# Two pairs of batch 1 prepared during batch 0's attention, and element-wise work moved from GpSimd to VectorE

## The chip, the core and the metric

The kernel runs on one core of one Trainium2 chip. The metric is the device time of one execution in microseconds (us). A core has TensorE (PE in the profile; its weight loads are PEld), VectorE (DVE), ScalarE (ACT), GpSimd (POOL) and SyncE (SP), which here issues most of the DMAs. Each engine works through its own instructions in order; semaphores make one engine wait for another.

## The reference, cut to what matters

Three layers run one after the other on 2 batches of 768 tokens. The first is a linear attention with a decaying state (8 heads of 48), the second adds the real part of a two-dimensional Fourier transform and a normalised two-layer network, the third is a gated network with a mixing over tokens.

```
for t in range(S):                                   # attention, per batch and head
    cur = np.einsum('bhd,bhe->bhde', u[None] * kt, vt)
    y[:, :, t] = np.einsum('bhd,bhde->bhe', rt, state + cur)
    state = wt[:, :, :, None] * state + np.einsum('bhd,bhe->bhde', kt, vt)
...
X = np.fft.fft(np.fft.fft(x, axis=1), axis=2)        # first network
u = x + np.real(X)
un = (u - mean(u)) / np.sqrt(var(u) + 1e-06)
x = u + np.maximum(un @ w_ch1, 0.0) @ w_ch2
...
h = gelu(x @ w_in); u, v = halves(h)                 # second network
v_n = (v - mean(v)) / np.sqrt(var(v) + 1e-06) * g_ln
out = x + (u * (w_sg @ v_n + b_sg)) @ w_out
```

## The kernel before, in words

**Pairs.** Attention is done for a pair of heads at a time: n = 0 to 3 are the pairs of batch 0, n = 4 to 7 those of batch 1. A pair's 768 tokens are cut in 6 chunks of 128. `prep` loads a pair (decays into `P`, receptance and key into `rk`, values into `v`) and makes the scaled operands: the running product of the decays is a scan on VectorE (L232), its reciprocal comes from a logarithm and an exponential on ScalarE (L238, L239), then follow four products over 112x768: receptance (L245), key (L247), a check sum (L249) and a correction of the key (L250). The rooms of odd pairs are called `prk`, `XE` and `XO`, those of even pairs `P` and `rk`.

**Own term.** Each token's own contribution `dv` is values times a number per head, `dg`. For batch 0 `dg` is a matmul into PSUM (`dg_ps`) of the product made in L243, copied by ScalarE (L274). For batch 1 it is two products of 128x576 (L264, L266) and a reduction on VectorE (L267). L279 multiplies the values by it.

**Chain of a pair.** TensorE makes scores (`sc_ps`) and transposes the keys (`kn_ps`). ScalarE copies both; GpSimd masks the scores (L294, 128x384). The keys' copy `kn` goes into products with the values (`kv_ps`), ScalarE copies these (L316), a scan on VectorE turns them into chunk states (L319) with the decays that ScalarE spread out into `dec` (L317), ScalarE writes the states `U` (L321), TensorE makes `y_ps`. L344 adds `dv`. `butterfly` (L349, L350) adds and subtracts the halves of the sequence and splits the result in a high part on ScalarE (L351) and a low part (L352). The keys' copy, the chunk states and the butterfly share one buffer, `kn`.

**Weights.** They come as 64-bit numbers. `convert` makes 32-bit ones on VectorE (L170 to L172), `divide` rounds to a high part on ScalarE (L176) and subtracts for a low part `w` (L177). Matmuls run three passes over high and low parts.

**Stages.** Batch 0's attention comes first, then its Fourier transform. Then `merge` weaves batch 1's attention and transform with the first network on batch 0 (`z_ps`, `ch`; L531 makes the low part `z_lo`). From then on the first network on batch 1 and the second network follow. A scheduler orders each engine's instructions; `first_through` is the last VectorE instruction of batch 0's transform, and batch 1's scans, its first own products and the later weights' conversions are held behind it. `NP` is 4. In `attention` the line that calls `prep` ahead is L374 to L376: two pairs ahead, but only within the same batch. `KV` and `PV` name the pairs whose key product and own product are on VectorE rather than GpSimd; `TM` are the pairs whose own term is made of products.

## Time and profile before

| | before |
|---|---|
| median of 3 runs | 485.19 us (483.95 to 487.18) |
| the profiled execution: its time | 485.52 us |
| the profiled execution: its span | 483.7 us |
| mean granted TensorE clock | 0.947 |
| PE / PEld busy | 433.6 us (90%) / 408.3 us (84%) |
| DVE busy | 274.0 us (57%), 453 instructions |
| ACT busy | 172.7 us (36%) |
| POOL busy | 182.1 us (38%), 182 instructions |

The span is what the trace covers; 1.8 us of the execution lie around it. Busy shares are means over stages that differ: between 14.5 and 76.5 us is batch 0's attention, to 104.1 us its transform, to 216 us batch 1's attention woven with the first network, and from there TensorE is busy almost without a break.

### The profile page before, as it was taken

The page shows a single profiled execution, that of the slowest core. Times are in us where ns is not written, and L with a number is a line of the kernel's source. Part 1 is how long each engine was busy: PE and PEld are TensorE (multiplying, and loading weights), DVE is VectorE, ACT ScalarE, POOL GpSimd, SP SyncE. Part 2 cuts the span into 40 slices and gives each one's busy share as a digit, 9 for nine tenths or more (in the row PEclk, how much of TensorE's full clock was granted, in tenths as well). Part 3 has the DMA queues.
Part 4 walks back from the last instruction along what each step waited for, and adds up shares of the span by engine and source line. Part 5 has one row for each costly group of instructions (what it writes and reads, how often), then busy time and mean ns, then how long its engine had stood idle before and what let it go on. Part 6 is the DMA issues. An engine that isn't in the chain of part 4 may idle for free.

```text
span 483.7 us, 6884 instructions
## 1 busy us (share of the span) xinstructions
PE 433.6 (90%) x2662; PEld 408.3 (84%) x2662; DVE 274.0 (57%) x453; ACT 172.7 (36%) x369; POOL 182.1 (38%) x182
## 2 busy tenths in 40 slices
PE   8778788876789688999999799999998999999994
PEld 8667787765678678899999699999987998999994
DVE  4857387389986978634044963541158734711332
ACT  2435355452344236444322532431355413311110
POOL 2857553154786967320000341200446524200330
PEclk9659899897979989999999899999999999999998
DMA  8948534036035223013000041000243100110002
GB/s 213 251 146 265 166 119 130 0 101 242 0 119 176 91 67 110 1 40 91 1 0 2 1 131 33 1 0 1 66 114 88 61 1 1 43 56 1 0 20 87
DMA packets 14074, 36.75 MB, mean 76 GB/s; under 512 B 1808, under 2 KB 5680, under 8 KB 13648
## 3 DMA queue, kind: packets, MB, share of 16 engines
q1 hardware_dynamic: 13456, 32.54, 22.5%
q0 software_dynamic: 576, 3.68, 2.2%
q8 instruction: 23, 0.38, 0.3%
q14 instruction: 19, 0.16, 0.1%
HBM read 33.86 MB, written 2.36 MB: 75 GB/s over the span
## 4 chain that ended last, share of the span: by engine, by line
PE 55%; DVE 15%; issue 10%; POOL 6%; DMA 5%; ACT 4%; SPq 1%; POOLq 0%; ACTq 0%; DVEq 0%
PE s_ps L107 10%; PE ch L107 8%; PE z_ps L107 8%; PE o_ps L107 5%; PE u_ps L107 4%; PE d_ps L107 3%; PE x_ps L107 3%; PE v_ps L107 3%; PE t_ps L426 2%; PE y_ps L342 2%; DMA raw<-in_wsg 2%; DVE st L171 2%; DVE st L170 2%; DVE st L172 1%; DMA w_raw<-in_w 1%
## 5 line engine op out<-in xcount | busy, mean ns | idle before, releaser
L107 PE MATMUL ch<-z_hi,w 128*128 128x384 f32 x288 | 84.5, 355 | 3.9 <-DVE uT L541 2.3
L107 PE MATMUL z_ps<-us_hi,w 128*128 128x384 f32 x288 | 82.5, 348 | 0.8 <-ACT us_hi L506 0.5
L107 PEld LDWEIGHTS ch<-z_hi,w 128*128 128x128 f32 x288 | 55.4, 199 | 6.0 <-ACT z_hi L530 2.7
L107 PE MATMUL ch<-z_lo,w 128*128 128x384 f32 x144 | 51.3, 356 | 10.2 <-DVE z_lo L531 10.2
L531 DVE SCALAR_TENSOR_TENSOR z_lo<-z_ps,z_hi 128x384 fp32r<-128x384 f32 x48 | 26.4, 552 | 55.7 <-ACT z_hi L530 55.7
L107 PEld LDWEIGHTS z_ps<-us_hi,w 128*128 128x128 f32 x288 | 54.1, 193 | 2.2 <-ACT us_hi L506 0.8
L107 PE MATMUL z_ps<-us_lo,w 128*128 128x384 f32 x144 | 49.4, 343 | 0.0
L530 ACT ACTIVATE z_hi<-z_ps 128x384 fp32r<-128x384 f32 x48 | 23.4, 490 | 57.0 <-PE z_ps L107 43.8
L107 PEld LDWEIGHTS ch<-z_lo,w 128*128 128x128 f32 x144 | 28.5, 198 | 12.4 <-DVE z_lo L531 12.1
L623 POOL TENSOR_TENSOR vn_lo<-t_g,vn_hi 128x384 fp32r<-128x384 f32 x16 | 16.1, 1014 | 57.1 <-ACT vn_hi L622 57.1
L619 DVE SCALAR_TENSOR_TENSOR t_g<-s_ps,g,bsg 128x384 f32<-128x384 f32 x16 | 9.5, 615 | 43.6 <-PE s_ps L107 43.6
L294 POOL TENSOR_SCALAR_AFFINE_SELECT sc<-sc 128x384 f32<-128x384 f32 x32 | 29.5, 939 | 12.0 <-ACT sc L293 12.0
L342 PE MATMUL y_ps<-v,sc 128*128 128x120 f32 (+1 forms) x192 | 34.0, 301 | 0.0
L177 POOL TENSOR_TENSOR w<-st,w 128x384 fp32r<-128x384 f32 (+1 forms) x18 | 24.4, 1363 | 24.0 <-ACT w L176 23.9
L107 PE MATMUL s_ps<-wsg_hi,vn_lo 128*128 128x384 f32 x96 | 32.3, 336 | 0.0
L107 PE MATMUL s_ps<-wsg_hi,vn_hi 128*128 128x384 f32 x96 | 32.3, 336 | 0.0
L107 PE MATMUL s_ps<-wsg_lo,vn_hi 128*128 128x384 f32 x96 | 32.3, 336 | 0.0
L483 POOL TENSOR_TENSOR z_lo<-uc,z_hi 128x384 fp32r<-128x384 f32 x7 | 7.8, 1120 | 60.0 <-ACT z_hi L482 59.9
L342 PEld LDWEIGHTS y_ps<-v,sc 128*128 128x128 f32 x192 | 28.6, 209 | 1.2 <-issue 0.8
L107 PEld LDWEIGHTS z_ps<-us_lo,w 128*128 128x128 f32 x144 | 27.9, 194 | 0.0
L177 POOL TENSOR_TENSOR wsg_lo<-raw,wsg_hi 128x384 fp32r<-128x384 f32 x12 | 12.4, 1038 | 33.2 <-ACT wsg_hi L176 33.2
L622 ACT CAST vn_hi<-t_g 128x384 fp32r<-128x384 f32 x16 | 8.0, 513 | 38.9 <-DVE t_g L620 28.0
(261 smaller groups left out, 1060.0 us busy)
## 6 DMA issues: line engine op xcount, KB each, us to landing
raw<-in_w SPq DMA_DIRECT2D x12, 384.0 KB, 3.4
w_raw<-in_w SPq DMA_DIRECT2D x12, 384.0 KB, 4.5
raw<-in_win SPq DMA_DIRECT2D x8, 384.0 KB, 3.8
prod<-in_ruk SPq DMA_DIRECT2D x4, 624.0 KB, 4.6
tdft<-in_tdft POOLq DMA_DIRECT2D x2, 1158.0 KB, 6.8
v<-in_v SPq DMA_DIRECT2D x8, 288.0 KB, 5.7
raw<-in_wsg SPq DMA_DIRECT2D x12, 192.0 KB, 2.4
out<-o SPq DMA_DIRECT2D x12, 192.0 KB, 1.9
```

The costliest lines, as they stand in the source:

```text
L107: nc.tensor.matmul(o, lhsT=x, rhs=y, start=start and i == 0, stop=stop and i == len(ps) - 1, **kw)
L170: behind(nc.vector.tensor_scalar(out=st, in0=top, scalar1=3, scalar2=0x3FFFFFF8, op0=ALU.logical_shift_left, op1=ALU.bitwise_and), first_t ...
L171: nc.vector.scalar_tensor_tensor(out=st, in0=top, scalar=0xC0000000, in1=st, op0=ALU.bitwise_and, op1=ALU.bitwise_or)
L177: nc.gpsimd.tensor_tensor(out=w.lo[to], in0=x, in1=w.hi[to].bitcast(F32), op=ALU.subtract)
L294: nc.gpsimd.affine_select(out=sc, in_=sc, pattern=[[0, 3], [1, C]], compare_op=ALU.is_gt, fill=0.0, base=0, channel_multiplier=-1)
L342: nc.tensor.matmul(y3[:, i, to], lhsT=sc[h][:, i, :], rhs=vf[:, of], start=c == 0, stop=True, skip_group_check=c > 0)
L426: nc.tensor.matmul(o, lhsT=l, rhs=r, start=i == 0, stop=i == len(parts) - 1)
L530: nc.scalar.activation(out=z.hi, in_=z_ps, func=AF.Relu)
L531: nc.vector.scalar_tensor_tensor(out=z.lo, in0=z_ps, scalar=0.0, in1=z.hi.bitcast(F32), op0=ALU.max, op1=ALU.subtract)
L619: nc.vector.scalar_tensor_tensor(out=t, in0=s_ps[h], scalar=g[:, f:f + 1], in1=bsg[:, hs], op0=ALU.mult, op1=ALU.add)
L622: nc.scalar.copy(vn.hi[:, f, 3 * h:3 * h + 3], th)
L623: nc.gpsimd.tensor_tensor(out=vn.lo[:, f, 3 * h:3 * h + 3], in0=th, in1=vn.hi[:, f, 3 * h:3 * h + 3].bitcast(F32), op=ALU.subtract)
```

## The change

It does six things.

1. The first two pairs of batch 1, n = 4 and 5, are prepared during batch 0's attention: `prep` may now run past the batch's end (the loop's last bound is `len(pairs)`, and n = 2 and 3 look three pairs ahead), and only scans from n = 6 on (`NP + AP`), and own products from n = 5 on, stand behind `first_through`. That needs a fourth `ends` buffer.
2. All key products (L247 before) are on VectorE; before, those of n = 2 to 7 were on GpSimd.
3. Batch 1's own products (L264, L266 before) are on VectorE, and so is the product with the values (L279) of all pairs. For batch 0 it reads `dg_ps` in PSUM directly; the copy by ScalarE is gone.
4. The low parts of all weights (L177 before) are on VectorE.
5. `dec` has no buffer of its own any more: it lies beside the chunk states in the `kn` buffer and is written 112x288 wide, so it can be written only after the `kv_ps` matmuls have read `kn`.
6. GpSimd keeps the masks, batch 0's products of pairs 1 to 3 in L243, the butterflies' low parts and small work of the networks.

```diff
-KV = range(2)
+KV = range(8)
+AP = 2
-PV = range(1)
+PV = (0, *range(4, 8))
...
     def divide(w, to, x):
         nc.scalar.copy(w.hi[to], x)
-        nc.gpsimd.tensor_tensor(out=w.lo[to], in0=x, in1=w.hi[to].bitcast(F32), op=ALU.subtract)
+        nc.vector.tensor_tensor(out=w.lo[to], in0=x, in1=w.hi[to].bitcast(F32), op=ALU.subtract)
...
-            if b:
+            if n >= NP + AP:
                 behind(scan, first_through)
...
-        ends = all_ends[n % 3]
+        ends = all_ends[n % 4]
...
             own = (nc.vector if n in PV else nc.gpsimd).tensor_tensor(out=r, in0=r, in1=k, op=ALU.mult)
-            behind(own, first_through, mybir.DependencyClass.Sync)
-            nc.gpsimd.tensor_tensor(out=r, in0=r, in1=u.to_broadcast([C, NC_, 2 * D]), op=ALU.mult)
+            if n >= NP + AP - 1:
+                behind(own, first_through)
+            nc.vector.tensor_tensor(out=r, in0=r, in1=u.to_broadcast([C, NC_, 2 * D]), op=ALU.mult)
...
-        nc.scalar.copy(dg[:, :, :, 0], dg_ps[:, :2 * NC_].rearrange("p (c h) -> p c h", h=2))
-        times_v(dv, dg, v)
+        times_v(dv, dg_ps[:, :2 * NC_].rearrange("p (c h o) -> p c h o", h=2, o=1), v)
...
     def times_v(dv, dg, v):
-        nc.gpsimd.tensor_tensor(out=dv.rearrange("p c (h e) -> p (c h) e", h=2), in0=v.rearrange("p c (h e) -> p (c h) e", h=2),
+        nc.vector.tensor_tensor(out=dv.rearrange("p c (h e) -> p (c h) e", h=2), in0=v.rearrange("p c (h e) -> p (c h) e", h=2),
...
-        us = ap([PR, D, NC_], "kn")
+        both = ap([PR, 2, D, NC_], "kn")
+        us, dec = both[:, 0], both[:, 1]
+        nc.scalar.copy(dec, ends[:, None, :].to_broadcast([PR, D, NC_]))
         nc.scalar.copy(us, kv_ps[:, :NC_ * D].rearrange("p (c e) -> p e c", c=NC_))
-        nc.scalar.copy(dec[:, :, 0:NC_ - 1], ends[:, None, 0:NC_ - 1].to_broadcast([PR, D, NC_ - 1]))
...
-            for m in range(len(ready) + n, min(n + (3 if n == 0 else 2), (b + 1) * NP)):
+            for m in range(len(ready) + n, min(n + (3 if n in (0, NP - 2, NP - 1) else 2), len(pairs))):
```

The scheduler makes new orders of this. Line numbers after the change are 2 or 3 higher than before. On VectorE in the middle of batch 0's attention the order before was this, from pair 3's scan (`XO`) on; `kn` are chunk states and butterflies of the pairs before it:

```order
L232 SCALAR_TENSOR_TENSOR XO<-XO,d_91 112x774
L319 SCALAR_TENSOR_TENSOR kn<-kn,dec 112x288
L344 TENSOR_TENSOR dv<-y_ps,dv 128x288
L245 SCALAR_TENSOR_TENSOR XO<-XO 112x768
L349 TENSOR_TENSOR kn<-dv 128x288
L350 TENSOR_TENSOR kn<-dv 128x288
L344 TENSOR_TENSOR dv<-y_ps,dv 128x288
L249 SCALAR_TENSOR_TENSOR y_379,unit<-XO,y_379 112x768
L250 SCALAR_TENSOR_TENSOR XO<-y_379,XO 112x768
L319 SCALAR_TENSOR_TENSOR kn<-kn,dec 112x288
L344 TENSOR_TENSOR dv<-y_ps,dv 128x288
```

After the change pair 4 (`P`, `rk`) and its own products (`prod`) stand there, ahead of and around the next chunk states:

```order
L252 SCALAR_TENSOR_TENSOR XO<-y_377,XO 112x768
L234 SCALAR_TENSOR_TENSOR P<-P,d_91 112x774
L347 TENSOR_TENSOR dv<-y_ps,dv 128x288
L247 SCALAR_TENSOR_TENSOR rk<-rk,P 112x768
L249 TENSOR_TENSOR rk<-rk,y_396 112x768
L251 SCALAR_TENSOR_TENSOR y_396,unit<-P,y_396 112x768
L266 TENSOR_TENSOR prod<-prod 128x576
L322 SCALAR_TENSOR_TENSOR kn<-kn 112x288
L252 SCALAR_TENSOR_TENSOR rk<-y_396,rk 112x768
L269 TENSOR_TENSOR prod<-prod 128x576
```

So pair 3's next chunk states no longer follow its keys directly: pair 4's scan and products come in between.

The second place is VectorE at the start of the woven stage, right after batch 0's last transform rows (`uT`). Before, it was pair 4 that was prepared there:

```order
L232 SCALAR_TENSOR_TENSOR P<-P,d_91 112x774
L671 TENSOR_TENSOR unit<-unit 112x1
L496 TENSOR_TENSOR uc<-uT_84 128x384
L531 SCALAR_TENSOR_TENSOR z_lo<-z_ps,z_hi 128x384
L245 SCALAR_TENSOR_TENSOR rk<-rk,P 112x768
L531 SCALAR_TENSOR_TENSOR z_lo<-z_ps,z_hi 128x384
L497 TENSOR_TENSOR uc<-uc,uT_84 128x384
L267 TENSOR_REDUCE dg<-prod 128x12
L170 TENSOR_SCALAR st<-w_raw 128x768
```

After, the scan there is pair 6's, the two products `prod` are pair 5's own term, and the low part of a weight (L179) follows its conversion at once:

```order
L234 SCALAR_TENSOR_TENSOR P<-P,d_91 112x774
L266 TENSOR_TENSOR prod<-prod 128x576
L674 TENSOR_TENSOR unit<-unit 112x1
L499 TENSOR_TENSOR uc<-uT_84 128x384
L269 TENSOR_TENSOR prod<-prod 128x576
L500 TENSOR_TENSOR uc<-uc,uT_84 128x384
L534 SCALAR_TENSOR_TENSOR z_lo<-z_ps,z_hi 128x384 x2
L270 TENSOR_REDUCE dg<-prod 128x12
L172 TENSOR_SCALAR st<-w_raw 128x768
L281 TENSOR_TENSOR dv<-v,dg 128x576
L173 SCALAR_TENSOR_TENSOR st<-w_raw,st 128x768
L174 SCALAR_TENSOR_TENSOR st<-w_raw,st 128x768
```

The first `z_lo` now has two products more ahead of it, and pair 4's products are gone from this place.

## Rows read from the trace of the kernel before

**Rows 1.** Windows: us; busy (xcount) PE, PEld, DVE, ACT, POOL; PEclk; DMA share, GB/s
```profile
14.50:76.50 62.00, 50.35 (x383) 44.23 (x383) 43.26 (x53) 27.00 (x59) 39.77 (x36) 0.81 0.63 187
...
104.10:193.70 89.60, 68.61 (x432) 60.25 (x432) 77.92 (x89) 35.92 (x74) 63.87 (x42) 0.90 0.37 122
193.70:216.00 22.30, 21.12 (x166) 19.73 (x165) 11.62 (x27) 9.60 (x21) 6.36 (x8) 1.00 0.02 2
```

**Rows 2.** Waits of PE, 104.1 to 193.7 us: total us, times, longest us
```profile
PE ch L107 <- DVE z_lo L531: 9.7, 5, 3.0
PE sc_ps L290 <- DVE rk L250: 4.7, 1, 4.7
```

**Rows 3.** Waits of DVE in the same stretch
```profile
DVE st L170 <- POOL w L177: 5.1, 4, 2.8
```

**Rows 4.** Timeline of DVE: start us, us, then the instruction
```profile
105.97 1.29 DVE L671 TENSOR_TENSOR unit<-unit 112x1 f32<-112x1 f32 x1
...
116.66 0.94 DVE L250 SCALAR_TENSOR_TENSOR rk<-y,rk 112x768 f32<-112x768 f32 x1
...
168.32 2.92 DVE L250 SCALAR_TENSOR_TENSOR rk<-y,rk 112x768 f32<-112x768 f32 x1
```

**Rows 5.** Timeline of POOL
```profile
104.44 2.80 POOL L264 TENSOR_TENSOR prod<-prod 128x576 f32<-128x576 f32 x1 [0.83 <-DVE uT L459]
...
208.67 0.99 POOL L294 TENSOR_SCALAR_AFFINE_SELECT sc<-sc 128x384 f32<-128x384 f32 x2 [1.50 <-ACT sc L293]
```

**Rows 6.** Groups of DVE, 104.1 to 193.7 us: form, xcount | busy us, mean ns | idle before
```profile
L171 DVE SCALAR_TENSOR_TENSOR st<-w_raw,st 128x768 uint32<-128x768 uint32 x6 | 8.4, 1406 | 0.1
...
L531 DVE SCALAR_TENSOR_TENSOR z_lo<-z_ps,z_hi 128x384 fp32r<-128x384 f32 x12 | 6.6, 546 | 1.4 <-ACT z_hi L530 1.4
L170 DVE TENSOR_SCALAR st<-w_raw 128x768 uint32<-128x768 uint32 x6 | 6.5, 1078 | 2.3 <-POOL w L177 2.3
...
L232 DVE TENSOR_TENSOR_SCAN prk<-prk,d 112x774 f32<-112x774 f32 x2 | 3.5, 1758 | 0.0
```

**Rows 7.** Groups of POOL in the same stretch that stay on POOL
```profile
L294 POOL TENSOR_SCALAR_AFFINE_SELECT sc<-sc 128x384 f32<-128x384 f32 x12 | 12.4, 1050 | 2.5 <-ACT sc L293 2.5
...
L352 POOL TENSOR_TENSOR AL<-kn,AH 128x576 fp32r<-128x576 f32 x2 | 3.5, 1772 | 3.3 <-ACT AH L351 3.3
L483 POOL TENSOR_TENSOR z_lo<-uc,z_hi 128x384 fp32r<-128x384 f32 x2 | 2.1, 1072 | 2.4 <-ACT z_hi L482 2.4
```

**Rows 8.** Groups of ACT, 104.4 to 205 us
```profile
L176 ACT CAST w<-st 128x768 fp32r<-128x768 f32 x6 | 5.0, 832 | 17.2 <-DVE st L172 17.2
...
L317 ACT COPY dec<-ends 112x240 f32<-112x240 f32 x4 | 1.5, 383 | 0.0
```

**Rows 9.** Waits of DVE, 14.5 to 76.5 us
```profile
DVE dv L344 <- PE y_ps L342: 9.7, 3, 5.3
DVE kn L319 <- ACT kn L316: 3.7, 1, 3.7
```

**Rows 10.** Groups of DVE, 14.5 to 76.5 us
```profile
L232 DVE TENSOR_TENSOR_SCAN prk<-prk,d 112x774 f32<-112x774 f32 x1 | 4.5, 4483 | 0.0
...
L247 DVE TENSOR_TENSOR prk<-prk,AL 112x768 f32<-112x768 f32 x1 | 2.5, 2500 | 0.9 <-ACT AL L239 0.9
...
L352 DVE TENSOR_TENSOR AL<-kn,AH 128x576 fp32r<-128x576 f32 x1 | 0.8, 757 | 0.5 <-ACT AH L351 0.5
```

**Rows 11.** Groups of POOL, 14.5 to 76.5 us, that leave POOL
```profile
L279 POOL TENSOR_TENSOR dv<-v,dg 128x576 f32<-128x576 f32 x4 | 5.3, 1328 | 1.8 <-DVE kn L350 1.8
L177 POOL TENSOR_TENSOR w<-st,w 128x384 fp32r<-128x384 f32 x4 | 4.5, 1135 | 4.3 <-ACT w L176 4.3
...
L247 POOL TENSOR_TENSOR XO<-XO,y 112x768 f32<-112x768 f32 x1 | 1.5, 1540 | 0.0
```

**Rows 12.** Windows of two later stretches, columns as in rows 1
```profile
260.00:279.00 19.00, 15.75 (x81) 14.37 (x81) 17.93 (x38) 8.94 (x21) 5.60 (x5) 0.91 0.01 1
360.00:380.00 20.00, 18.20 (x100) 17.10 (x99) 17.93 (x34) 11.45 (x24) 11.94 (x17) 1.00 0.36 99
```

More of the change, by code (lines that the diff above doesn't have):

```diff
@@ L850, in fused @@
         states = [sh.tile([PR, NC_ - 1, 2 * D], F32, name=f"U{i}") for i in range(2)]
-        all_ends = [sh.tile([PR, NC_], F32, name=f"ends{i}") for i in range(3)]
-        dec = sh.tile([PR, D, NC_], F32, name="dec")
-        for t in (*states, *all_ends, dec):
+        all_ends = [sh.tile([PR, NC_], F32, name=f"ends{i}") for i in range(4)]
+        for t in (*states, *all_ends):
             nc.gpsimd.memset(t, 0.0)
```

## The prediction

> **What bounds the kernel now.** The page's slices come first: TensorE is busy nearly everywhere after 216 us, so a change to other engines can only pay ahead of that. The windows view then cuts the front into stages [rows 1]. From 104.1 to 193.7 us, where batch 1's four pairs are prepared beside the first network, VectorE is busy 77.9 of 89.6 us and TensorE 68.6, at a mean granted clock of 0.90: VectorE is the fuller one. The waits view shows which way it goes: TensorE stands 9.7 us for `z_lo`, which VectorE makes late, and 4.7 us for pair 4's keys [rows 2]. VectorE itself stands 5.1 us for GpSimd's low parts, which must be read before the conversion buffer can be written again [rows 3]. From 193.7 to 216 us TensorE is busy 21.1 of 22.3 us. In batch 0's attention, 14.5 to 76.5 us, VectorE is busy 43.3 of 62 us, and its long waits are for `y_ps` (9.7 us) and for the copy of `kv_ps` (3.7 us) [rows 1, 9]: there it is a link in the pairs' chain, not full.
>
> The second thing to see is that VectorE's busy time is not all work. The same product takes 0.94 us at 116.66 and 2.92 us at 168.32 [rows 4]. L671, one number per partition, takes 1.29 us, and it ends just when GpSimd's L264 (104.44 to 107.24) does [rows 4, 5]. So the two engines hold each other up. I set each VectorE group of the stretch against its shortest instance (0.94 for 768 wide, 1.75 for a scan). L171 has 6 instances at 1.41, which gives 2.7 us too much (shortest 0.95), L170 6 at 1.08 against its shortest, 0.53, gives 3.3 [rows 6]. Over the 16 groups that show it that makes 23.5 us of the 77.9. The same working gives 13.0 us of 43.3 in batch 0's attention, of which pair 1's scan (4.48 against 1.75) and key product (2.50 against 0.94) are 4.3 [rows 10].
>
> **The change part by part.**
>
> *The woven stage, 104.1 to 193.7.* Undisturbed, VectorE's work there is 77.9 - 23.5 = 54.4 us. By the two orders it loses two preparations (2 scans of 1.75, 6 products of 0.94), one reduction, one `z_lo` and one half conversion: 3.5 + 5.7 + 0.75 + 0.55 + 0.55, about 11.1. It gains 6 low parts 768 wide and 2 of 384, 2 key products, 6 own products and 3 products with the values. These VectorE has not done before in these forms, so their price goes by width: 0.94 for 768 [rows 4], 0.55 for 384 [rows 6], and 0.76 for 576, the time of the one butterfly low part that VectorE makes [rows 10]. That makes 5.6 + 1.1 + 1.9 + 4.6 + 2.3, about 15.3. Net +4.2, so 58.6 us. What GpSimd still costs: before, 63.9 us of its busy time went with 23.5 us of excess, 0.37 us per us. Of its groups masks, low parts of butterflies and column sums stay, 12.4 + 3.5 + 2.1 = 18.0 us [rows 7], so 18.0 x 0.37 = 6.6 us. VectorE would be busy 65.2 us.
>
> Its idle time was 89.6 - 77.9 = 11.7 us. The 5.1 us of waits for GpSimd go. New ones come: at two places a low part follows its conversion at once, so VectorE, in order, stands for ScalarE's cast of 0.83 us [rows 8], and everything behind it, `z_lo` among it, stands too: +1.7. Idle 8.3, the stretch 73.5 us, a gain of 16.1. This is above the 68.6 us that TensorE was busy there, so TensorE does not bind yet; the floor of this term is a gain of 89.6 - 68.6 = 21. What is late next is `z_lo` again, at the start, with two own products ahead of it.
>
> *Batch 0's attention.* VectorE undisturbed has 43.3 - 13.0 = 30.3 us. Added are pair 4 and 5's preparations (2 scans, 6 products: 9.1), 4 key products (3.8; two of them pair 4's and 5's), 3 instructions of pair 4's own term (2.3), 4 products with the values (3.0), and 4 low parts of 384 whose casts fall ahead of the end (2.2): 20.4, so 50.7. GpSimd loses 5.3 + 4.5 + twice 1.5 [rows 11] and keeps 27 of its 39.8 us; at 13.0 / 39.8 = 0.33 us per us that is 8.8 of excess. VectorE would be busy 59.5 of the old 62 us. Before, 18.7 us were idle. The waits of 9.7 and 3.7 us [rows 9] are the cover under which pairs 4 and 5 hide; they are real time in the chain of the pairs, so part of them remains. `dec` now waits for `kv_ps` and stands on the chain, about 0.4 us for each of 4 pairs [rows 8]. With 6 us left idle the stretch is 65.5, with 10 it is 69.5. I take 7.5: 67, or +5. Bounds: nothing added if the chain is shortened by the GpSimd work that leaves it; +16 if the old idle time all stays.
>
> *DMAs.* Pair 4's and 5's loads are issued in this stage either way (the order of SP has the same loads, one 338 KB load of `P` earlier); nothing is priced.
>
> *The transform, 76.5 to 104.1, and 193.7 to 216.* TensorE leads there and the added low parts (4 and 2 of 0.55) fall where VectorE waits: zero, with 1 us as the bound.
>
> *From 216 on.* 18 to 22 low parts of 384 move to VectorE. It has room except in two stretches where it is busy 17.9 of 19 us and 17.9 of 20 us, and TensorE stands beside it (15.8 and 18.2 busy) [rows 12]. In the first 4 low parts (2.2 us) come in front of the sums that free `ch`, while some GpSimd interference leaves. In the second 6 low parts (3.3 us) and a conversion that stood later come ahead of the last `vn_lo`, with 2.1 us idle to take them. I take +2; bounds -1 and +5.
>
> Sum against the profiled execution's own 485.5: +5 - 16 + 2 = -9, so **476.5 us**. The median of the runs shown is 0.3 lower than that execution, which is within what they scatter.
>
> A rule weighed: GpSimd's remaining masks run against a VectorE that now has far more two-input instructions. The rows give 0.37 us of hold-up per us of GpSimd [rows 1, 7]. The Trainium skill, "SBUF — State Buffer", section "Who interferes with whom", says that a VectorE instruction with two SBUF inputs and a GpSimd instruction that reads SBUF share a port under an exclusive lock, held for the whole instruction, and that the loser blocks fully. By that rule the remaining 18 and 27 us could cost VectorE up to 1 us each instead of 0.37 and 0.33, and the sum would be about 506. The rows agree in kind (L671 above), but not with a collision every time.
>
> **The rivals.** *Most of it comes back in batch 0 (same).* VectorE stands in order for each `y_ps` and copy as before, so 14 us stay idle there instead of 7.5: 73.5 us, +11.5, and 485.5 + 11.5 - 16 + 2 = 483. For it: those waits come from the pairs' chain, not from GpSimd. Against it: before, pair 2's products stood behind the longest one, 5.3 us [rows 9], and by the new order its key product and correction come earlier.
>
> *The masks hold up a full VectorE (slower).* One mechanism, both stages: as VectorE rests less, each us of GpSimd costs it r instead of 0.35. The time is 476.5 + 45 (r - 0.35), with 45 = 18 + 27 us left on GpSimd. It equals the old time at r = 0.55 and is 1% slower from r = 0.66, so 491 or more. For it: the rule above, and pair 1's scan, stretched from 1.75 to 4.48 under continuous GpSimd work [rows 10]. Against it: a mask undisturbed is 0.5 us [rows 5], half its busy mean, so the measured 18 us are already stretched.
>
> *More than that (faster).* VectorE's idle time falls to 4 in the woven stage and TensorE sets the pace: -20.5; batch 0 +2.5; later 0: 467.5.
>
> That the change does not do what it says can be left out: the orders show pairs 4 and 5 in batch 0's attention and no low part of a weight on GpSimd.
>
> **How the numbers follow.** Forecast (470 to 480.3) 0.55, more than that 0.07, most comes back 0.25, slower 0.13. About 1% is what a measurement of this kernel can tell from no change: faster is 0.55 + 0.07 = 0.62, within 1% is 0.25, slower 0.13. The range runs from the better rival, 467, into the case of "same", 488; above it lies most of the slower rival, below it little.
>
> **What would show it.** Right: GpSimd busy near 90 us (half), VectorE's L250 near 0.94 in the woven stage, pair 4's scores before the first `ch`, the stretch from batch 0's last transform row to pair 7's keys near 74 us, batch 0's attention ending 3 to 8 us later. Wrong: that stretch above 82 us with VectorE busy above 75 (the masks), or above 82 with VectorE idle 12 or more (the chain); batch 0's attention 12 us later; a new wait of TensorE in the last 270 us beyond 5 us.

## The result and the profile after

The changed kernel takes **469.51 us** (median; 467.92 to 474.93) against 485.05 for the kernel before: a ratio of 0.9694, with an interval of 0.961 to 0.978. Measured once more beside other kernels it took 470.67 us, ratio 0.970 (0.964 to 0.976). The forecast was 476.5 us with a range of 467 to 488: the direction was right, the time lies in the range, and the gain of 15.5 us is larger than the 9 that were summed.

| | before | after |
|---|---|---|
| profiled execution: time / span | 485.52 / 483.7 us | 468.76 / 466.8 us |
| mean granted TensorE clock | 0.947 | 0.958 |
| TensorE busy / idle in the span | 433.6 / 50.1 us | 427.9 / 38.9 us |
| VectorE busy | 274.0 us | 284.0 us |
| GpSimd busy | 182.1 us | 93.7 us |

GpSimd lost 88 us of busy time, and VectorE, which took that work, got only 10 more. The windows view of the changed kernel (us; busy (xcount) of PE, PEld, DVE, ACT, POOL; granted clock; DMA share, GB/s) has batch 0's attention, the woven stretch up to pair 7's keys, and what follows up to batch 1's first transform row; the first two answer to [rows 1]:

```profile
15.40:78.60 63.20, 49.10 (x382) 43.26 (x382) 57.16 (x81) 30.87 (x64) 26.51 (x25) 0.87 0.65 195
106.82:174.58 67.76, 58.75 (x407) 52.16 (x405) 62.39 (x96) 30.07 (x60) 13.55 (x15) 0.95 0.44 147
174.58:225.20 50.62, 50.45 (x330) 48.99 (x330) 20.30 (x45) 21.36 (x51) 8.29 (x9) 0.93 0.11 32
```

The woven stretch fell from 89.4 to 67.8 us, and GpSimd is busy 13.6 us in it instead of 63.9. Its waits (total us, times, longest), first of TensorE, then of VectorE, answering to [rows 2, 3]:

```profile
PE ch L109 <- DVE z_lo L534: 5.5, 4, 3.2
```

```profile
DVE w L179 <- ACT w L178: 2.5, 2, 1.6
DVE rk L247 <- DMA rk<-in_rk: 1.2, 1, 1.2
DVE prk L234 <- DMA prk<-in_wx: 0.7, 1, 0.7
DVE prod L266 <- DMA prod<-in_ruk: 0.4, 1, 0.4
```

TensorE's wait for pair 4's keys is gone, that for `z_lo` fell from 9.7 to 5.5. VectorE's wait for GpSimd's low parts is gone too; in its place it stands 2.5 us for ScalarE's casts and 2.3 us for loads. VectorE's timeline shows the two key corrections of the stretch (0.94 and 2.92 before, [rows 4]) and the product of one number per partition that took 1.29 us before:

```profile
109.14 0.15 DVE L674 TENSOR_TENSOR unit<-unit 112x1 f32<-112x1 f32 x1
...
147.96 0.94 DVE L252 SCALAR_TENSOR_TENSOR rk<-y,rk 112x768 f32<-112x768 f32 x1
...
173.64 0.94 DVE L252 SCALAR_TENSOR_TENSOR prk<-y,prk 112x768 f32<-112x768 f32 x1
```

All kernels below are cut at the same four events on VectorE: the low part of batch 0's last butterfly (end of **S1**), batch 0's last transform row (**S2**), pair 7's corrected keys (**S3**, the woven stretch), and the end (**S4**). "Hold-up" is one measure for all: each VectorE instruction's time less that of the shortest instance of its line and shape in any run, summed over S1 (from 15 us) and S3. The names are those of the experiments. The medians are of all executions; the ratios leave out, as slow, executions over 1.5% above the fastest of their kernel: one of one_early (678.6 us at a mean clock of 0.556), one of late_low_back_same, three of the kernel before beside the first four experiments, and the one of low_back_same that its stages are read from.

| kernel | median us | ratio (95%) | S1 | S2 | S3 | S4 | hold-up S1, S3 | GpSimd busy S1, S3 |
|---|---|---|---|---|---|---|---|---|
| before | 485.05 | 1 | 76.4 | 27.9 | 89.4 | 290.0 | 11.2, 25.0 | 39, 64 |
| after | 469.51 | 0.969 (0.961 to 0.978) | 78.6 | 28.2 | 67.8 | 292.2 | 8.6, 6.8 | 27, 14 |
| after_again | 470.67 | 0.970 (0.964 to 0.976) | 81.7 | 28.1 | 68.2 | 293.4 | 8.3, 6.5 | 30, 14 |
| early_only | 486.64 | 1.0055 (1.002 to 1.009) | 90.3 | 28.0 | 74.5 | 293.0 | 18.7, 18.1 | 49, 50 |
| no_early | 475.10 | 0.977 (0.969 to 0.985) | 72.4 | 27.8 | 86.7 | 288.6 | 7.0, 5.9 | 25, 17 |
| low_back_same | 475.50 | 0.976 (0.966 to 0.985) | 82.9 | 28.2 | 70.1 | 294.4 | 8.1, 10.3 | 32, 28 |
| products_back_same | 480.76 | 0.990 (0.982 to 0.998) | 86.0 | 28.9 | 70.4 | 293.5 | 16.6, 15.6 | 47, 35 |
| late_low_back_same | 470.49 | 0.966 (0.958 to 0.975) | 80.0 | 28.2 | 68.4 | 292.8 | 8.9, 6.6 | 30, 15 |
| extra_two | 478.96 | 0.988 (0.982 to 0.994) | 86.5 | 27.8 | 70.0 | 293.1 | 14.4, 10.2 | 47, 33 |
| extra_one | 474.60 | 0.980 (0.974 to 0.986) | 81.3 | 28.3 | 69.1 | 293.9 | 9.9, 7.8 | 46, 30 |
| one_early | 472.47 | 0.976 (0.969 to 0.983) | 72.5 | 28.0 | 75.4 | 290.4 | 7.0, 4.4 | 26, 16 |
| pairs_off | 463.72 | 0.956 (0.949 to 0.962) | 76.2 | 28.3 | 65.5 | 292.3 | 2.7, 4.1 | 18, 12 |
| masks_left | 459.27 | 0.950 (0.942 to 0.958) | 74.2 | 28.5 | 65.0 | 291.1 | 2.8, 2.9 | 18, 8 |
| masks_no_early | 470.34 | 0.970 (0.965 to 0.975) | 70.6 | 28.0 | 82.4 | 289.7 | 2.5, 3.4 | 12, 12 |

The stages come from one execution each (and GpSimd's times in S1 from 15 us on), and S1 must be read with care. after_again is the changed kernel once more:

> The changed kernel once more, beside the runs it is compared with. Both theories: 468 to 472, batch 0's attention 78 to 80 us, the woven stretch 67 to 69.

Here is the whole of S1 in the two executions, first after, then after_again:

```profile
0.00:78.60 78.60, 60.15 (x465) 53.75 (x465) 66.61 (x96) 35.55 (x73) 31.01 (x43) 0.89 0.69 201
```

```profile
0.00:81.70 81.70, 65.72 (x465) 59.31 (x465) 66.71 (x96) 35.70 (x73) 33.74 (x43) 0.81 0.65 193
```

The same 465 matmuls take 60.2 us at a granted clock of 0.89 and 65.7 at 0.81, and S1 is 3.1 us longer, above the 78 to 80 that were expected. S3 repeats within half a microsecond.

### The profile page after: what moved, and what is told of

Read it like the earlier page. It is cut to its first block, busy times and chain, and to the rows that moved or that the text cites. A ratio compares the mean times of both kernels' runs of the same rounds, so it can differ in the third digit from the quotient of the medians.

```text
span 466.8 us, 6863 instructions
## 1 busy us (share of the span) xinstructions
PE 427.9 (92%) x2662; PEld 405.1 (87%) x2662; DVE 284.0 (61%) x517; ACT 173.0 (37%) x365; POOL 93.7 (20%) x118
## 5 line engine op out<-in xcount | busy, mean ns | idle before, releaser
L109 PE MATMUL ch<-z_hi,w 128*128 128x384 f32 x288 | 82.8, 348 | 5.3 <-ACT z_hi L533 2.8
L109 PE MATMUL z_ps<-us_hi,w 128*128 128x384 f32 x288 | 81.5, 344 | 0.0
L296 POOL TENSOR_SCALAR_AFFINE_SELECT sc<-sc 128x384 f32<-128x384 f32 x32 | 25.4, 812 | 66.4 <-ACT sc L295 66.3
L109 PEld LDWEIGHTS ch<-z_lo,w 128*128 128x128 f32 x144 | 28.3, 196 | 8.7 <-DVE z_lo L534 8.7
L345 PE MATMUL y_ps<-v,sc 128*128 128x120 f32 (+1 forms) x192 | 32.4, 296 | 0.0
L345 PEld LDWEIGHTS y_ps<-v,sc 128*128 128x128 f32 x192 | 27.6, 205 | 0.9 <-issue 0.7
L109 PE MATMUL x_ps<-tdft,AH 128*128 128x386 f32 (+1 forms) x72 | 19.3, 350 | 6.0 <-ACT AH L354 6.0
L109 PEld LDWEIGHTS x_ps<-tdft,AH 128*128 128x128 f32 x72 | 13.0, 192 | 6.5 <-ACT AH L354 6.5
```

Of the source, the lines that this page charges most:

```text
L109: nc.tensor.matmul(o, lhsT=x, rhs=y, start=start and i == 0, stop=stop and i == len(ps) - 1, **kw)
L296: nc.gpsimd.affine_select(out=sc, in_=sc, pattern=[[0, 3], [1, C]], compare_op=ALU.is_gt, fill=0.0, base=0, channel_multiplier=-1)
L345: nc.tensor.matmul(y3[:, i, to], lhsT=sc[h][:, i, :], rhs=vf[:, of], start=c == 0, stop=True, skip_group_check=c > 0)
```

## The experiments

### Which part of the change pays

Two theories stood against each other. *Relief*: VectorE is the bound of the woven stretch; GpSimd's work stretches its instructions, so taking that work off and taking two preparations out each help there, and what the second costs in batch 0's attention depends on GpSimd. *Early preparation is the whole gain* was the main rival.

**early_only**: the early preparation alone (`AP` is 2), every operation on its old engine.

```diff
-            if b:
+            if n >= NP + AP:
                 behind(scan, first_through)
...
-            behind(own, first_through, mybir.DependencyClass.Sync)
+            behind(own, first_through if n >= NP + AP - 1 else None, mybir.DependencyClass.Sync)
...
-            for m in range(len(ready) + n, min(n + (3 if n == 0 else 2), (b + 1) * NP)):
+            for m in range(len(ready) + n, min(n + (3 if n in (0, NP - 2, NP - 1) else 2), len(pairs))):
```

> The kernel before with the early preparation of pairs 4 and 5 alone; every operation stays on the engine it had. Theory (VectorE's hold-ups by GpSimd in the woven stage are most of the gain, and early preparation only moves work): the woven stage loses two preparations, 11 us of undisturbed VectorE work, and some 14 us of GpSimd work, but batch 0's attention gets both, with GpSimd busy over 50 of its 62 us; woven stretch about 74 us (before 89.4), batch 0's attention 8 to 13 us longer, total 478 to 484. Rival A (early preparation is the whole gain): 468 to 473, woven stretch near 68. Rival B (alone it gives nothing): 485 or more.

Measured: 486.64 us, ratio 1.0055 (1.002 to 1.009): **no gain**, if anything a loss of half a per cent. The total of 478 to 484 that the theory expected is missed, and rival B's 485 or more came out. The windows of S1 (from 15 us) and S3, and two waits of VectorE in S1:

```profile
15.00:90.34 75.34, 53.65 (x382) 46.95 (x382) 59.15 (x69) 31.40 (x68) 49.05 (x42) 0.80 0.53 168
118.38:192.92 74.54, 61.27 (x401) 54.01 (x399) 58.98 (x72) 29.40 (x60) 49.72 (x35) 0.88 0.40 134
```

```profile
DVE dv L344 <- PE y_ps L342: 10.1, 4, 5.6
DVE y L249 <- POOL rk L247: 2.8, 1, 2.8
```

The woven stretch does what the theory says (74.5 us), but batch 0's attention gets 13.9 us longer, a little more than the 8 to 13 expected. VectorE still stands 10.1 us for `y_ps`, as before [rows 9], so the pairs' work did not go under that wait; hold-up rose from 11.2 to 18.7; and pair 4's key product, still on GpSimd, makes VectorE stand 2.8 us, with everything that is queued behind the check sum (L249).

**no_early**: the changed kernel with `AP = 0` and the old look-ahead.

```diff
-AP = 2
+AP = 0
...
-            if n >= NP + AP - 1:
+            if n >= NP:
...
-            for m in range(len(ready) + n, min(n + (3 if n in (0, NP - 2, NP - 1) else 2), len(pairs))):
+            for m in range(len(ready) + n, min(n + (3 if n == 0 else 2), (b + 1) * NP)):
```

> The changed kernel with the early preparation taken back: the element-wise work stays on VectorE. Theory: VectorE has 14 us more undisturbed work in the woven stretch than in the changed kernel, and its hold-ups stay small (about 5 us): stretch 80 to 83 us instead of 67.8; batch 0's attention 2 to 4 us shorter; total 478 to 482. Rival A (early preparation is the whole gain): 485 or more. Rival C (taking the work off GpSimd is the whole gain): 468 to 473.

Measured: 475.10 us, ratio 0.977. Its windows of S1 and S3:

```profile
15.00:72.37 57.37, 51.78 (x380) 46.38 (x380) 42.11 (x60) 26.90 (x57) 25.09 (x26) 0.80 0.65 199
100.13:186.81 86.68, 68.85 (x433) 60.44 (x433) 78.85 (x121) 37.54 (x75) 16.79 (x18) 0.89 0.39 126
```

Better than expected, and elsewhere than expected. In the woven stretch hold-up fell from 25.0 to 5.9 us, but VectorE is busy 78.9 us as before (77.7): the moved work filled the place of the hold-ups, and the stretch gains 2.7 us only, where 6 to 9 were expected. Batch 0's attention gains 4.0. So neither half explains the whole: early preparation alone gains nothing, moving the work alone gains 2.3%, both gain 3.0%. Early preparation takes 14.9 us from the woven stretch with GpSimd at its old work and 18.9 without; what it costs in S1 differs more, 13.9 us and 6.2 to 9.3.

**low_back_same** and **products_back_same** put parts of the work back on GpSimd. The scheduler would have ordered all engines anew, so in these two (and in the later runs whose names end so, and the two with added work) the changed kernel's order is written into the kernel: every instruction that stays on its engine keeps its place.

```diff
     def divide(w, to, x):
         nc.scalar.copy(w.hi[to], x)
-        nc.vector.tensor_tensor(out=w.lo[to], ...)
+        nc.gpsimd.tensor_tensor(out=w.lo[to], ...)
```

> The changed kernel with the low parts of all weights on GpSimd again; every other instruction keeps the place that it has in the changed kernel on its engine (the order is written into the kernel). Theory: in the woven stretch VectorE loses 8.5 us of work, but 16 us of GpSimd work come back and hold VectorE up by 0.37 us per us, 6 us, and VectorE stands some 3 to 5 us for GpSimd's reading of the conversion buffer: stretch 1 to 5 us longer; 348 to 383 us of before again 2 us longer; total 472 to 477. Rival (low parts on GpSimd were most of the loss): 480 or more. Rival (they are worth nothing): 468 to 471.

Measured: 475.50 us, ratio 0.976. Its S3 window, and a wait of VectorE in it:

```profile
111.08:181.21 70.13, 58.97 (x407) 51.84 (x405) 60.20 (x88) 29.63 (x60) 28.49 (x24) 0.96 0.41 142
```

```profile
DVE st L172 <- POOL w L179: 6.4, 5, 2.8
```

The signs are as expected: 2 us more in the woven stretch, with the wait of [rows 3] back (6.4 us) and 3.6 us more of hold-up against 8 us less work. They come from its longest execution (477.3 us); the granted clock of S3 is 0.96 there, as in the changed kernel (0.95), but that of S1 0.77, so nothing is read from its S1 of 82.9. The interval (0.966 to 0.985) overlaps with the changed kernel's, so what the low parts cost in all is not shown.

```diff
-KV = range(8)
+KV = range(2)
...
-PV = (0, *range(4, 8))
+PV = range(1)
...
-            nc.vector.tensor_tensor(out=r, in0=r, in1=u.to_broadcast([C, NC_, 2 * D]), op=ALU.mult)
+            nc.gpsimd.tensor_tensor(out=r, in0=r, in1=u.to_broadcast([C, NC_, 2 * D]), op=ALU.mult)
...
-        nc.vector.tensor_tensor(out=dv.rearrange(...
+        nc.gpsimd.tensor_tensor(out=dv.rearrange(...
```

> The changed kernel with the key products of pairs 2 to 7, batch 1's own products and the products with the values on GpSimd again (and the copy of batch 0's numbers per head on ScalarE); every other instruction keeps its place. Theory: in the woven stretch VectorE loses 9 us of work, GpSimd gets 23 us, which hold VectorE up by some 8 us, and GpSimd's two products of 2.8 us stand on the way of each pair's values: stretch 2 to 6 us longer; batch 0's attention, where GpSimd becomes busy 55 of 63 us, 3 to 6 us longer; total 474 to 481. Rival (these products are hidden anyway): 468 to 471.

Measured: 480.76 us, ratio 0.990, two thirds of the gain given back. S1 is 86.0 us, 4 to 7 above the changed kernel; its window and that of S3:

```profile
15.00:85.99 70.99, 52.98 (x368) 47.77 (x368) 56.30 (x71) 31.25 (x66) 46.95 (x37) 0.78 0.57 177
114.84:185.24 70.40, 59.51 (x403) 52.80 (x403) 63.92 (x84) 29.72 (x60) 34.84 (x26) 0.92 0.42 141
```

VectorE executes 495 instructions in this kernel and 517 in the changed one, and is busy as long, 285.0 and 284.0 us: hold-ups of 16.6 and 15.6 us stand where its work stood. These products are the costly part of the moved work: in the woven stretch they raise GpSimd's time by 21 us and hold-up by 9, the low parts theirs by 14 and 3.6. Most of the time comes back in batch 0's attention.

**late_low_back_same**: only the second network's low parts back on GpSimd; `divide` gets the engine as an argument.

```diff
-            load_split(w, src, o, o, ...)
+            load_split(w, src, o, o, ..., nc.gpsimd)
```

> The changed kernel with the low parts of the second network's weights alone on GpSimd again (they are made after 200 us); every other instruction keeps its place. The prediction's term (on VectorE they cost 2 us): 466 to 468.5. The reading of the two profiles (TensorE's idle time from 348 us on fell from 1.8 us to nothing with them on VectorE): 471 to 473, with TensorE waiting again near 350 us of this run.

Measured: 470.49 us, ratio 0.966 (0.958 to 0.975) against 0.970 (0.964 to 0.976): no difference, and the interval, 8 us wide, is too wide to tell the two readings (466 to 468.5, 471 to 473) apart. The windows between batch 1's first transform row and the second network's gate, of this run and then of the changed kernel:

```profile
226.47:369.68 143.21, 138.49 (x778) 132.85 (x778) 75.53 (x155) 53.37 (x111) 39.39 (x44) 1.00 0.15 42
```

```profile
224.91:367.12 142.21, 138.80 (x778) 134.62 (x778) 82.98 (x178) 53.95 (x111) 16.71 (x20) 0.99 0.14 42
```

TensorE is busy 138.5 and 138.8 us with the same 778 matmuls, and S4 is 292.8 us, between the 292.2 and 293.4 of the changed kernel: where these low parts are made makes no difference there that shows.

**one_early**: pair 4 alone prepared early.

```diff
-AP = 2
+AP = 1
...
-            for m in range(len(ready) + n, min(n + (3 if n in (0, NP - 2, NP - 1) else 2), len(pairs))):
+            for m in range(len(ready) + n, min(n + (3 if n == 0 else 2), len(pairs))):
```

> The changed kernel with one pair of batch 1 (pair 4) prepared during batch 0's attention instead of two. By the runs with and without the early preparation the two pairs cost batch 0's attention 6 to 9 us and take 19 us from the woven stretch. Theory (the woven stretch, near TensorE's own pace over most of its length with both, has VectorE as its bound again with one): woven stretch 74 to 78 us, batch 0's attention 75 to 77, total 471 to 475. Rival (the first pair is enough, the second only costs batch 0): 464 to 469.

Measured: 472.47 us, ratio 0.976 (0.969 to 0.983), S1 72.5, S3 75.4. The time is where the theory put it, the woven stretch too; S1 is shorter than expected, at a granted clock of 0.91. The intervals of one and of two pairs overlap, so the second pair's worth is not shown by this run alone.

### What GpSimd's work costs VectorE

The prediction's slower rival said that each us of masks would cost a full VectorE 0.66 us or more; it had used 0.33 to 0.37 for all GpSimd work. Two runs add GpSimd instructions that nothing waits for, 32 each, behind every pair of masks, to a scratch tile, in the changed kernel's order (`ident3` stands for the first 104 columns of the identity, read three times; extra_two adds the first line, extra_one the second, each twice).

```diff
+            nc.gpsimd.tensor_tensor(out=scr, in0=ident3, in1=ident3, op=ALU.mult)
+            nc.gpsimd.affine_select(out=scr, in_=ident3, pattern=[[0, 3], [1, 104]], ...)
```

> The changed kernel with 32 more GpSimd instructions that nothing waits for: behind every pair of masks two products of two SBUF inputs, 128x312, written to a scratch tile; every other instruction keeps its place. It measures the price of GpSimd's work for VectorE by itself. They should take GpSimd 25 to 35 us, half in each attention. Theory (a product of two inputs on GpSimd holds VectorE up by about half its time, as the changed kernel's remaining ones show: 4.3 us beside VectorE, 2.5 us of hold-up): 5 to 8 us of hold-up more in each stage, 8 to 15 in all, and as VectorE is nearly full there, 475 to 481. Rival (an exclusive lock for whole instructions): 12 us and more in each stage, 485 or more. Rival (GpSimd's work is free for VectorE, what helped was the order alone): 468 to 472.

> As the run with two more products behind every pair of masks, but the 32 added instructions are masks of one SBUF input, 128x312, on the same scratch tile. Theory (the masks that stay cost VectorE little: in the changed kernel's woven stretch 0.8 us of hold-up beside 5.5 us of masks): 1 to 2 us of hold-up more in each stage, 469 to 473. The prediction's slower rival (each us of mask costs a full VectorE 0.66 us or more): 6 us and more in each stage, 478 or more. A price as in the kernel before, 0.35: 472 to 477.

The group of the added instructions on GpSimd and the S3 window, of extra_two and then of extra_one:

```profile
L297 POOL TENSOR_TENSOR scr<-ident 128x312 f32<-128x312 f32 x32 | 37.5, 1171 | 1.3
```

```profile
114.31:184.33 70.02, 59.60 (x407) 52.56 (x405) 65.99 (x94) 29.86 (x60) 32.51 (x27) 0.96 0.42 142
```

```profile
L297 POOL TENSOR_SCALAR_AFFINE_SELECT scr<-ident 128x312 f32<-128x312 f32 x32 | 34.6, 1080 | 1.1
```

```profile
109.53:178.63 69.10, 60.48 (x407) 53.54 (x405) 63.63 (x95) 29.96 (x60) 29.53 (x27) 0.92 0.43 144
```

Products of two inputs: 37.5 us of GpSimd's time raised hold-up by 6.0 us in S1 and 3.5 in S3 (against the mean of the changed kernel's two profiles), **0.25 us per us**, and the kernel by 1.8%, 8 us. Masks of one input: 34.6 us raised it by 1.4 and 1.1, **0.07 us per us**. The slower rival is refuted for the masks: it needed 0.66. The median of extra_one rose by 1.0% all the same, 4 us (the intervals overlap), more than its hold-up of 2.6 and more than the theory's 473; where the rest went is open, since its stages lie within or 1 us above those of the changed kernel's two profiles.

What makes the two prices differ takes a closer look, since GpSimd's time holds its own standing as well. Here are all added instructions (ns, shortest/median/longest) and VectorE's product of one number per partition, first of extra_two, then of extra_one:

```profile
L297 POOL TENSOR_TENSOR scr<-ident x32: 695/902/2862, 18.7 to 199.5; 128x312 f32<-128x312 f32 x32
...
116.62 0.66 DVE L674 TENSOR_TENSOR unit<-unit 112x1 f32<-112x1 f32 x1
```

```profile
L297 POOL TENSOR_SCALAR_AFFINE_SELECT scr<-ident x32: 457/1060/2635, 19.1 to 192.9; 128x312 f32<-128x312 f32 x32
...
111.84 0.41 DVE L674 TENSOR_TENSOR unit<-unit 112x1 f32<-112x1 f32 x1
```

Undisturbed an added product takes 0.70 us and an added mask 0.46; the rest of their means (1.17 and 1.08) is GpSimd's own delay. L674, 0.15 us in the changed kernel, loses 0.51 us to a product and 0.26 to a mask. It is one of many: of the VectorE instructions that overlap added instructions and no other work of GpSimd, 15 lose more than 0.1 us to products and 14 to masks, most of them 0.51 to 0.56 us and 0.26 to 0.30, whether they are 1 or 774 wide; those that take an input from PSUM (`z_lo`, L347) lose 0.03 us at most. Meetings are as many with either kind, and one costs some 0.2 us less than the GpSimd instruction takes undisturbed. So the shorter masks are cheaper by their length already; that the number of inputs matters is not shown, as no run adds instructions of one length that differ in it alone.

### A version that beats both

If GpSimd's work of two inputs is the costly part, what the change left of it there should go as well: **pairs_off** moves batch 0's products of pairs 1 to 3 and the low parts of the butterflies, **masks_left** the first network's column sums too, so that GpSimd keeps the masks there (the last two pairs of lines are masks_left's alone; the last edit stands twice).

```diff
-PV = (0, *range(4, 8))
+PV = range(8)
...
-            butterfly(..., nc.vector if b == 0 and p == NP - 1 else nc.gpsimd)
+            butterfly(..., nc.vector)
...
-            nc.gpsimd.tensor_tensor(out=parts.lo, in0=x, ...)
+            nc.vector.tensor_tensor(out=parts.lo, in0=x, ...)
-            nc.gpsimd.tensor_tensor(out=ucs[0], in0=ucs[0], ...)
+            nc.vector.tensor_tensor(out=ucs[0], in0=ucs[0], ...)
```

> The changed kernel with the rest of GpSimd's products of two inputs in the first two layers on VectorE too (batch 0's products of pairs 1 to 3, the low parts of all butterflies, the first network's column sums); GpSimd keeps the masks. Theory (these hold VectorE up by about 0.3 to 0.5 us per us and stand on the way of TensorE's matmuls, and VectorE makes each in half the time): in batch 0's attention VectorE takes 3 products of 0.94 and 3 low parts of 0.75, 5 us, and loses some 6 us of hold-up; in the woven stretch 3 to 4 us either way: 464 to 469. Rival (VectorE is full now, more work makes it later): 472 to 478.

> As the run in which GpSimd keeps the masks alone, but the first network's column sums stay on GpSimd: only batch 0's products of pairs 1 to 3 and the low parts of the butterflies move to VectorE. Theory: batch 0's attention 1 to 3 us shorter, the woven stretch as in the changed kernel: 466 to 470. Rival (VectorE is full): 472 or more.

Measured: masks_left 459.27 us, ratio **0.950** (0.942 to 0.958); pairs_off 463.72, ratio 0.956 (0.949 to 0.962). Both are faster than expected, and masks_left is clear of the changed kernel. Its busy times, then its windows of S1 and S3:

```profile
PE 429.1 (94%) x2662; PEld 407.9 (89%) x2662; DVE 284.4 (62%) x542; ACT 171.9 (37%) x365; POOL 60.9 (13%) x93
```

```profile
15.00:74.17 59.17, 52.02 (x382) 46.15 (x382) 53.65 (x83) 30.22 (x63) 18.05 (x18) 0.80 0.65 203
102.70:167.66 64.96, 56.65 (x405) 51.21 (x403) 60.72 (x98) 28.91 (x58) 8.36 (x10) 0.97 0.45 153
```

VectorE has 25 instructions more than in the changed kernel and is busy as long (284.4 and 284.0 us): hold-up is down to 2.8 and 2.9 us. S1 is 4.4 and 7.5 us shorter than in the changed kernel's two profiles.

**masks_no_early** takes the early preparation out of that kernel, by the edit of no_early.

> The kernel in which GpSimd keeps the masks alone, with the early preparation taken back. With the kernel before (no offload), the changed one and the one with masks alone it gives the worth of early preparation at three amounts of GpSimd work: in the kernel before it costs 2 us, in the changed kernel it brings 5. Theory (its price is paid in batch 0's attention, and lies in the hold-ups and queues that GpSimd's products make there; without them it is nearly covered by VectorE's waits): early preparation brings more here, 8 to 12 us, so 467 to 472 without it, batch 0's attention 70 to 72 us and the woven stretch 82 to 85. Rival (its worth does not hang on GpSimd): 462 to 465.

Measured: 470.34 us, ratio 0.970 (0.965 to 0.975), as the theory said. So early preparation is worth nothing (-0.55%) with all of GpSimd's products in place, about +0.7% in the changed kernel (the intervals overlap) and +2.0% (11 us by the medians; the intervals are apart) with the masks alone. The windows of S1 and S3:

```profile
15.00:70.56 55.56, 49.80 (x382) 44.57 (x382) 43.42 (x73) 27.07 (x57) 12.19 (x18) 0.82 0.67 206
98.57:180.99 82.42, 68.09 (x424) 59.10 (x422) 75.65 (x117) 34.18 (x68) 11.95 (x12) 0.89 0.40 133
```

Its price in S1 is now 3.6 us (70.6 to 74.2), for VectorE work of 10 us: most of it goes under VectorE's waits, which the prediction had called the cover.

## Why the prediction was right, step by step

**What bounds the kernel: right.** VectorE led in the woven stretch, and hold-ups by GpSimd were a third of its busy time there: they went from 25.0 to 6.8 us when the work left. Three signs named came out: GpSimd busy 93.7 us, L252 at 0.94, pair 4's scores at 103.3 us before the first `ch` at 110.0. Two came out in part: the woven stretch is 6 us below its 74, and batch 0's attention ends 2.2 us later in one execution and 5.3 in the other, where 3 to 8 were named.

**The chances.** The median of 469.51 lies just below the band of 470 to 480.3 that had 0.55, the second measurement's 470.67 just inside. In the woven stretch the faster rival, given 0.07, was nearer (20.5 us less and 4 us idle; measured 21.6 and 5.4), in the rest the forecast was.

**The woven term: right in kind, 5 us too small.** Forecast 73.5, measured 67.8 and 68.2. By the one measure above, VectorE's own work went from 52.7 to 55.6 us (+2.9; summed +4.2), hold-up to 6.8 and 6.5 (summed 6.6), idle time to 5.4 (summed 8.3). The hold-up came out by luck: the four low parts that stay there cost more than 0.37 us per us (masks_left, without their 6.8 us, has 2.9 us of hold-up, 3.8 less), the masks less. Of the 5.5 us that the gain was short, the largest miss is the idle time with 2.9; the change in own work and the fall of the hold-up miss by 1.3 each. Of the 11.7 us the prediction kept all but the waits for GpSimd's low parts, 6.6 us, and hardly any of that is left. These waits of before, 4.7 us, are 0.2 us after:

```profile
DVE kn L349 <- ACT U L321: 2.1, 2, 1.0
DVE z_lo L531 <- ACT z_hi L530: 1.4, 2, 0.8
DVE kn L319 <- ACT kn L316: 1.2, 1, 1.2
```

Against them stand the 2.3 us for loads, which the prediction priced at nothing, and casts of 2.5 us where 1.7 was summed.

**TensorE's floor of 68.6 us: wrong.** TensorE's busy time in a stretch is not a constant. It fell to 58.8 us, in part because it makes 407 matmuls there instead of 432, in part because the granted clock rose from 0.90 to 0.95. The 25 matmuls stand in S2 and S4 now; here are both stages, before and then after:

```profile
76.43:104.32 27.89, 25.73 (x157) 24.04 (x157) 16.40 (x40) 13.20 (x35) 6.01 (x6) 0.94 0.11 29
193.74:483.70 289.96, 277.44 (x1610) 268.85 (x1609) 129.58 (x264) 91.78 (x192) 69.63 (x81) 0.99 0.12 35
```

```profile
78.60:106.82 28.22, 26.19 (x167) 24.51 (x168) 16.21 (x39) 13.22 (x34) 3.08 (x4) 0.94 0.10 28
174.58:466.80 292.22, 282.78 (x1626) 274.67 (x1625) 138.76 (x291) 94.14 (x198) 46.09 (x57) 0.98 0.11 35
```

S2 has 10 more and S4 16. So 21.6 us less in S3 is not 21.6 us of gain: S4 is 2.2 longer.

**Batch 0's attention, +5: right.** It ends 2.2 us later in one execution and 5.3 in the other. The granted clock of the kernel before (0.81 from 15 us on) lies between those of the two (0.87 and 0.77), so the forecast of 5 is borne out, if not to the microsecond. In the first VectorE is busy 57.2 us and idle 6.0 (forecast 59.5 and 7.5). early_only shows what the term rests on: with GpSimd's products in place it is +13.9, the 11.5 of the rival "most of it comes back in batch 0" and more. That rival argued that the waits for `y_ps` come from the pairs' chain and not from GpSimd; in the changed kernel VectorE does not wait for `y_ps` in that stage (0.4 us in the second execution), while in no_early it does, and in early_only too (10.1 us, above). In these runs the pairs' work goes under that wait only once GpSimd's products are out of the way. VectorE's wait in no_early:

```profile
DVE dv L347 <- PE y_ps L345: 6.0, 3, 5.0
```

**`dec` on the chain, 0.4 us a pair: the rows agree**, in part. All instances of the copy (ns, shortest/median/longest) in the changed kernel, and what ScalarE waited for ahead of them:

```profile
L319 ACT COPY kn<-ends x8: 415/432/470, 21.6 to 183.9; 112x288 f32<-112x288 f32 x8
...
  PE kv_ps L315: 7.4, 3
```

ScalarE stood for `kv_ps` ahead of three of the eight, so there its 0.43 us is on the chain. A kernel with a buffer of its own for `dec` was not run.

**From 216 us on, +2: right number, wrong reason.** S4 is 2.2 us longer, but late_low_back_same, with the low parts back on GpSimd, has an S4 of 292.8, between the changed kernel's two, so they cost nothing that shows. What S4 has more is the 16 matmuls: TensorE is busy 5.3 us more there and idle 3.1 us less. That they are the whole reason is argued, as the clock is 0.98 instead of 0.99.

**The rule weighed.** extra_two and extra_one bear on the Trainium skill, "SBUF — State Buffer", section "Who interferes with whom". That GpSimd's reading holds VectorE up agrees in kind. The single meetings agree further than the prediction allowed: a VectorE instruction loses 0.51 us and more to a product of 0.70, and a product takes up to 2.86 us beside VectorE, so each stands for the other. What failed is the step from there to "up to 1 us each" (and to the 12 us a stage of extra_two's first rival): it took GpSimd's busy time for work, while much of that time is GpSimd's own standing. So 0.25 us per us does not speak against a lock, and the sum of about 506 was far off for that step.

**The sum.** In the profiled execution: +2.2 + 0.3 - 21.6 + 2.2 = -16.9 us of span; in the second one +5.3 + 0.2 - 21.2 + 3.4 = -12.3. Both are more than the forecast of -9, by 5 us of the woven term. In the first batch 0's attention adds another 2.8; in the second, at a lower clock in that stage, it does not, and S4 takes 1.4 back.

## What to carry to other kernels

Before work is moved under another engine's waits, look at what else slows the receiving engine there: the same early preparation gained nothing beside GpSimd's products and 2.0% once they were gone. Work on an engine that holds up the main one is paid twice, in its own time and in the main engine's: from the kernel before to masks_no_early GpSimd's busy time fell by 124 us, VectorE took that work and got 12 us busier, and the kernel 3.0% faster; early preparation then made that 5.0%. And a stage that got shorter is a gain only if it still does the same matmuls, so count them beside the time.

## What was not expected of the hardware

There is no one price of GpSimd's work for VectorE per us of its busy time, as the prediction took it: it was 0.25 for the added products, 0.07 for the added masks, and 0.55 for the low parts that masks_left takes from the woven stretch. Part of that busy time is GpSimd standing itself. The price of one meeting is steadier: mostly 0.51 to 0.56 us with a product that takes 0.70 undisturbed, and 0.26 to 0.30 with a mask of 0.46, for a VectorE instruction of any length.

One wait of TensorE can cost more than its length. The changed kernel's windows through the end of the woven stretch, and TensorE's timeline there (start us, us, instruction):

```profile
110.00:165.00 55.00, 52.52 (x381) 47.30 (x381) 49.63 (x73) 27.61 (x56) 12.59 (x14) 0.97 0.50 168
...
170.00:175.00 5.00, 2.61 (x8) 2.13 (x10) 5.00 (x12) 0.51 (x1) 0.00 (x0) 0.68 0.00 0
175.00:180.00 5.00, 4.84 (x32) 3.94 (x31) 1.30 (x5) 2.02 (x5) 0.99 (x2) 0.50 0.00 0
180.00:185.00 5.00, 5.00 (x36) 4.62 (x34) 2.16 (x5) 2.69 (x8) 0.00 (x0) 0.79 0.02 3
```

```profile
168.17 0.34 PE L109 MATMUL ch<-z_hi,w 128*128 128x384 f32 x1
...
172.37 0.69 PE L109 MATMUL ch<-z_lo,w 128*128 128x384 f32 x1 [3.17 <-DVE z_lo L534]
172.86 0.53 PE L109 MATMUL ch<-z_hi,w 128*128 128x384 f32 x1
...
180.54 0.52 PE L109 MATMUL z_ps<-us_lo,w 128*128 128x384 f32 x1
```

From 110 to 165 us TensorE is busy 52.5 of 55 us. Then VectorE makes pair 7's key product and check sum and parts of a weight's conversion ahead of a `z_lo`, TensorE stands 3.2 us, and behind that wait the clock is granted at 0.50, its level of 1.2 GHz, past 180 us: a matmul of 128x384 takes 0.52 to 0.53 us instead of 0.34. In after_again the same wait is 3.5 us, and the clock is at 0.50 from 177.5 to 184 us. Not every such wait does it: one of 3.2 us ahead of the `kv_ps` at 64.0 us of the changed kernel has the clock at 1.00 before and for 10 us behind it. The clock also differs between executions of one kernel, 0.81 and 0.89 in S1 of the changed kernel, beside 3 us of S1. Of the changed kernel's four timed executions the longest (474.9 us) had the lowest mean clock, 0.938, against 0.947 to 0.958 in the others.
